# Three VectorE instructions instead of four to convert a float64 weight, and another place for the ScalarE one

## The chip, the core and the metric

The kernel runs on one core of a Trainium2 chip. The metric is the device time of one execution in microseconds (us). TensorE (PE) multiplies, its weight loads are listed as PEld; VectorE is DVE, ScalarE is ACT, GpSimd is POOL, and SP is the sequencer that issues almost every DMA. Each engine works through its own instructions in order and waits on semaphores.

## What is computed

An attention with a learned relative bias (batch 4, 8 heads, 576 positions, head size 64), then a gated convolution block, then a block that mixes tokens with a cosine and a sine of a linear map:

```python
scores = scale * q @ k.T + bias           # bias: a small MLP of log-distances, per head
x = softmax(scores) @ v                   # reshaped to (4, 576, 512)
gate = sigmoid(causal_conv5(x, conv_w))
x = (gate * (x @ w_val)) @ w_out          # called m1 below
theta = x @ w_theta                       # from here on: m2
y = w_tok_r @ (x * cos(theta)) + w_tok_i @ (x * sin(theta))
u = x + y
out = u + relu(u @ w_ch)
```

The weights of the last two blocks arrive as float64: `w_val`, `w_out`, `w_theta`, `w_ch` are 512 x 512, `w_tok_r` and `w_tok_i` 576 x 576, `conv_w` is 5 x 512. Nothing is converted on the host; the kernel gets the 64-bit words as pairs of 32-bit integers.

## The kernel before

**Weight conversion.** `f64_stages` (L68) returns the stages of one block of 128 rows. `raw` holds the words, low and high alternating. Stage 0 loads it (SP, L706 or L717). Stage 1 is ACT: the absolute value of the high words read as float32, into `f64a` (L82). Stage 2 is DVE: it sets to zero what is below `TINY` and takes the sign back (L85). Stage 3 shifts left by 5 and right by 2 (DVE, L91), stage 4 ors in the two top bits (DVE, L96), stage 5 ors in the top three bits of the low words (DVE, L101). The float32 in `f64h` is then split into a high part (ACT, L105) and a low part (POOL, L108), stages 6 and 7. There are 12 blocks of 512 columns and one of 20 (`conv_w`) in the attention, 9 of 576 (the token weights, into `wtok`) in m1, and 8 of 256 (`w_ch`) in m2. `raw` and `f64a` have two buffers, `f64h` has one.

**Bias and attention.** First 36 groups of bias are made and written to DRAM, until about 57 us. The attention then runs over 80 steps; a step is one query tile of 128 rows of one pair of heads and one batch, five steps (four tiles and a tail of 64 rows) are an iteration, and there are 16 iterations. The first ten steps are taken in the order of `FIRST`. The order of instructions is written out by hand in `attention` (L419), under a manual schedule. At step s: PE makes the scores (`qk`, L242) into two PSUM tiles; DVE adds the bias and finds the minimum (`soft`, L256); ACT exponentiates (L259); one step later DVE and POOL normalise (`norm`, L268 to L271); three steps later PE transposes (L301, and L314 for the rest), ACT and DVE copy the result out (`tr_out`, `mid_out`, L279 and L281), and PE multiplies by the values (L362, L372). ACT copies the finished output (`xst`, L382).

**Places of the weight stages.** The table `WS` says in which step a stage of which block is written: (iterations after the block's own, step of the iteration counted from 0, stage, place in the step). Place 0 is ahead of `norm`, place 1 behind it, place 2 at the step's end. One block starts in each iteration, 13 in all.

**m1 and m2.** Four convolution taps per row block on DVE (L532), the gates (L564), splits into high and low parts (L63 on ACT, L65 on POOL), and matmuls in triples (L114 to L116); `xo` (L578) is the copy of an output out of PSUM by ACT, and `x2d` is where it is stored. The first taps already run in the last 18 steps of the attention. In m1, `pace` spreads the stages of the nine token blocks over 70 slots in the order in which they are listed; in m2, eight stages of the `w_ch` blocks are written behind each token product. A list scheduler sets the final order there. The first token block's load waits for the end of the attention.

Of the kernel before, what the change touches and what calls it, by code (L numbers as in the profile page):

```python
# [2 lines left out]

# [7 lines left out]
F32 = mybir.dt.float32  # L11
F32R = mybir.dt.float32r
I32 = mybir.dt.int32
AF = mybir.ActivationFunctionType
ALU = mybir.AluOpType
# [13 lines left out]
BW, BR = 592, 608  # L29
BIG = 3.0e38  # L30

TINY = struct.unpack("f", struct.pack("I", 0x38100000))[0]

MAGIC = 12582912.0
INV2PI = 0.15915494309189535
# [32 lines left out]
def f64_stages(nc, alloc, n, load, hi, lo):  # L68

    t = {}

    def s0():
        t["raw"] = alloc("raw")
        load(t["raw"])

    def s1():  # L80
        t["a"] = alloc("f64a")
        nc.scalar.activation(out=t["a"][:, :n], in_=t["raw"][:, :n, 1].bitcast(F32), func=AF.Abs)  # L82

    def s2():
        nc.vector.scalar_tensor_tensor(out=t["a"][:, :n], in0=t["a"][:, :n], scalar=TINY,  # L85
                                       in1=t["raw"][:, :n, 1].bitcast(F32), op0=ALU.is_ge, op1=ALU.mult)

    def s3():
        t["h"] = alloc("f64h")
        x, h = t["a"][:, :n].bitcast(I32), t["h"][:, :n].bitcast(I32)  # L90
        nc.vector.tensor_scalar(out=h, in0=x, scalar1=5, scalar2=2, op0=ALU.logical_shift_left,  # L91
                                op1=ALU.logical_shift_right)

    def s4():
        x, h = t["a"][:, :n].bitcast(I32), t["h"][:, :n].bitcast(I32)
        nc.vector.scalar_tensor_tensor(out=h, in0=x, scalar=-(1 << 30), in1=h, op0=ALU.bitwise_and,  # L96
                                       op1=ALU.bitwise_or)

    def s5():
        h = t["h"][:, :n].bitcast(I32)  # L100
        nc.vector.scalar_tensor_tensor(out=h, in0=t["raw"][:, :n, 0], scalar=29, in1=h,  # L101
                                       op0=ALU.logical_shift_right, op1=ALU.bitwise_or)

    def s6():
        nc.scalar.activation(out=hi, in_=t["h"][:, :n], func=AF.Copy)  # L105

    def s7():
        nc.gpsimd.tensor_tensor(out=lo, in0=t["h"][:, :n], in1=hi.bitcast(F32), op=ALU.subtract)  # L108

    return [s0, s1, s2, s3, s4, s5] + ([s6, s7] if lo is not None else []), t  # L110


def mm3(nc, out, wh, wl, xh, xl, first, last):
# [5 lines left out]
class Kernel:  # L119
# [270 lines left out]
    def av_plan(self, j):  # L390
# [13 lines left out]
        if qt < 3:  # L404
# [4 lines left out]

    WS = ((2, 0, 5, 2), (2, 1, 6, 2), (2, 2, 7, 2), (0, 2, 0, 2), (0, 4, 1, 2), (1, 2, 2, 1), (1, 4, 3, 0),
          (1, 4, 4, 1))

    BL = {(B - 2, 1): 0, (B - 2, 3): 1, (B - 2, 4): 4, (B - 1, 1): 2, (B - 1, 3): 3}

# [2 lines left out]
    def attention(self, blocks, hooks):  # L419
# [5 lines left out]
        for s in range(NU + 4):  # L425
# [38 lines left out]
            def stages(place):  # L464
                for i, step, stage, pl in self.WS:
                    if s < NU and r == step and pl == place and 0 <= it - i < len(blocks):
                        blocks[it - i][stage]()
# [236 lines left out]
    def wblock(self, alloc, dram, w, kc, c0=0, n=DM):  # L704
        def load(raw):
            self.nc.sync.dma_start(out=raw[:, :n].rearrange("p a b -> p (a b)"),  # L706
                                   in_=dram[128 * kc:128 * kc + 128, c0:c0 + n].bitcast(I32))
        return f64_stages(self.nc, alloc, n, load, w[0][:, kc, c0:c0 + n], w[1][:, kc, c0:c0 + n])[0]

    def tokblock(self, alloc, kt):  # L710
        wr, wi = self.a["w_tr"], self.a["w_ti"]

        def load(raw):
            flat = raw.rearrange("p a b -> p (a b)")
            if kt < 8:
                w, r = (wr, kt) if kt < 4 else (wi, kt - 4)
                self.nc.sync.dma_start(out=flat, in_=w[128 * r:128 * r + 128, :].bitcast(I32))  # L717
            else:
                self.nc.sync.dma_start(out=flat[0:64], in_=wr[TM:S, :].bitcast(I32))
                self.nc.sync.dma_start(out=flat[64:128], in_=wi[TM:S, :].bitcast(I32))  # L720
        return f64_stages(self.nc, alloc, S, load, self.wtok[0][:, kt], self.wtok[1][:, kt])[0]
# [22 lines left out]
    def conv_block(self, alloc):  # L744
        n = KC * 5

        def load(raw):
            for c in range(KC):
                self.nc.sync.dma_start(out=raw[:, 5 * c:5 * c + 5].rearrange("p k b -> p (k b)"),
                                       in_=self.a["conv_w"][128 * c:128 * c + 128, :].bitcast(I32))  # L750
        stages, t = f64_stages(self.nc, alloc, n, load, None, None)
        return stages + [lambda: self.nc.vector.tensor_copy(out=self.cw.rearrange("p c k -> p (c k)"),
                                                            in_=t["h"][:, :n]), lambda: None]
# [304 lines left out]
```

## Time and profile before

| what | us |
|---|---|
| median of 3 runs (lowest, highest) | 625.67 (624.54, 626.31) |
| the profiled execution, its own time | 622.14 |
| its span, first to last instruction | 620.4 |
| PE busy | 597.4 (96%) |
| PEld busy | 459.2 (74%) |
| DVE busy | 477.1 (77%) |
| ACT busy | 393.8 (63%) |
| POOL busy | 321.3 (52%) |
| the four conversion lines on DVE, all shapes, L85 / L91 / L96 / L101 | 20.7 / 19.0 / 21.9 / 22.2 |

The span can be cut into four stretches: bias (0 to 57), attention (57 to 288), m1 (288 to about 395), m2 (to 620). In a timeline row the first number is the start in us, the second the time; a bracket at the end tells how long the engine had been idle before and what ended that. A busy engine in one stretch may be idle in the next, so the shares of the whole span decide nothing.

### The profile page before, as it was taken

What the parts mean: (1) busy time and instruction counts of PE and PEld (TensorE: products, weight loads), DVE (VectorE), ACT (ScalarE), POOL (GpSimd) and SP (SyncE); (2) the same over time, 40 slices, a digit from 0 to 9 for tenths busy, and PEclk for the clock granted to TensorE, in tenths of its full rate; (3) what the DMA queues carried; (4) which work ended last, traced back from release to release, by engine and by line L of the source; (5) the groups of instructions that cost most, each with busy time, mean ns of one, the idle gap of its engine ahead of it and who ended that gap; (6) DMA issues with size and microseconds to landing.
All of it is one profiled execution on the core that took longest, in us unless ns stands there. A gap on an engine that the chain in (4) does not pass through costs nothing.

```text
span 620.4 us, 14765 instructions
## 1 busy us (share of the span) xinstructions
PE 597.4 (96%) x5552; PEld 459.2 (74%) x5552; DVE 477.1 (77%) x1155; ACT 393.8 (63%) x869; POOL 321.3 (52%) x342
## 2 busy tenths in 40 slices
PE   5999899999999998989999999999999999999997
PEld 2334455555555554557989999879998999999997
DVE  7997799999999998787999997499977436416112
ACT  5998788888888887976577574687447332614010
POOL 4555466666765665675577864244773242125120
PEclk9999899999999998999999999999999999999999
DMA  6999589569748963202555636331234003001002
GB/s 178 279 326 264 155 224 257 178 179 235 172 143 233 260 193 89 78 21 60 158 166 180 207 110 229 110 103 35 71 94 142 2 11 144 1 0 49 30 1 78
DMA packets 51975, 84.42 MB, mean 136 GB/s; under 512 B 7472, under 2 KB 32176, under 8 KB 51392
## 3 DMA queue, kind: packets, MB, share of 16 engines
q1 hardware_dynamic: 51728, 83.12, 45.8%
q8 instruction: 44, 0.72, 0.5%
q10 hardware_dynamic: 144, 0.30, 0.1%
q14 instruction: 27, 0.22, 0.1%
q0 software_dynamic: 32, 0.07, 0.0%
HBM read 58.39 MB, written 25.07 MB: 135 GB/s over the span
## 4 chain that ended last, share of the span: by engine, by line
PE 71%; DVE 9%; ACT 8%; DMA 7%; issue 3%; POOL 1%; SPq 0%; ACTq 0%; DVEq 0%
PE mm L114 12%; PE mm L116 12%; PE mm L115 12%; PE o L362 10%; PE s L242 10%; PE t L301 6%; PE bp L177 4%; DMA qr<-x1d 3%; DVE ns L256 2%; DVE gs L532 1%; ACT ev L187 1%; ACT e L259 1%; PE o L372 1%; DVE raw L532 1%; DMA scr<-ev 1%
## 5 line engine op out<-in xcount | busy, mean ns | idle before, releaser
L271 POOL TENSOR_SCALAR e<-e,ri 128x576 f32<-128x576 f32 x144 | 118.3, 832 | 83.0 <-DVE ri L269 29.9
L259 ACT ACTIVATE e<-ns,mx 128x576 f32<-128x576 f32 x144 | 111.1, 772 | 29.3 <-DVE mx L256 19.3
L256 DVE CUSTOM_DVE_ANT_0 ns<-s,bias 128x576 f32<-128x576 f32 x128 | 93.7, 750 | 9.1 <-PE s L242 6.5
L242 PE MATMUL s<-kr,qr 64*128 64x288 f32 (+1 forms) x640 | 94.7, 432 | 0.4 <-DVE mx L256 0.4
L116 PE MATMUL mm<-wtok,zl 128*128 128x288 f32 x288 | 84.7, 295 | 0.8 <-POOL zl L65 0.8
L114 PE MATMUL mm<-wtok,zh 128*128 128x288 f32 x288 | 84.7, 295 | 0.0
L115 PE MATMUL mm<-wtok,zh 128*128 128x288 f32 x288 | 84.6, 294 | 0.0
L362 PE MATMUL o<-et,vm 128*64 128x320 f32 (+1 forms) x512 | 77.9, 427 | 0.0
L65 POOL TENSOR_TENSOR ul<-x,uh 128x288 fp32r<-128x288 f32 x32 | 26.8, 837 | 89.3 <-ACT uh L63 68.8
L301 PEld LDWEIGHTS t<-idt,e 64*128 64x128 f32 x1152 | 42.8, 140 | 38.5 <-POOL e L271 20.0
L680 DVE TENSOR_TENSOR x<-mm,x 128x288 f32<-128x288 f32 x32 | 14.5, 454 | 63.3 <-PE mm L116 63.3
L362 PEld LDWEIGHTS o<-et,vm 128*64 128x64 f32 x512 | 31.7, 138 | 38.5 <-issue 18.9
L279 ACT ACTIVATE et<-t 128x512 f32<-128x512 f32 (+1 forms) x103 | 53.7, 544 | 8.8 <-PE s L314 7.0
L242 PEld LDWEIGHTS s<-kr,qr 64*128 64x128 f32 (+1 forms) x640 | 47.6, 179 | 15.7 <-DVE mx L256 6.4
L63 ACT ACTIVATE uh<-x 128x288 fp32r<-128x288 f32 x32 | 14.1, 441 | 68.3 <-DVE x L680 68.3
L301 PE MATMUL t<-idt,e 64*128 64x64 f32 x1152 | 53.7, 230 | 2.3 <-ACT et L279 2.2
L116 PEld LDWEIGHTS mm<-wtok,zl 128*128 128x128 f32 x288 | 54.0, 188 | 1.0 <-POOL zl L65 1.0
L115 PEld LDWEIGHTS mm<-wtok,zh 128*128 128x128 f32 x288 | 54.0, 188 | 0.1
L114 PEld LDWEIGHTS mm<-wtok,zh 128*128 128x128 f32 x288 | 54.0, 188 | 0.1
L532 DVE SCALAR_TENSOR_TENSOR gs<-qr,cw,gs 128x288 f32<-128x288 f32 (+4 forms) x96 | 45.9, 510 | 3.2 <-ACT gs L528 3.2
L177 PE MATMUL bp<-h,w2n 128*32 128x512 f32 (+48 forms) x648 | 43.9, 404 | 2.4 <-DVE h L164 1.5
L164 DVE TENSOR_SCALAR h<-wpsi,nbp_i 128x577 f32<-128x577 f32 (+35 forms) x108 | 45.2, 494 | 0.0
(130 smaller groups left out, 1551.1 us busy)
## 6 DMA issues: line engine op xcount, KB each, us to landing
scr<-ev SPq DMA_DIRECT2D x36, 296.0 KB, 4.9
qr<-in_q SPq DMA_DIRECT2D x32, 288.0 KB, 4.6
bias<-scr SPq DMA_DIRECT2D x32, 288.0 KB, 7.5
vm<-in_v SPq DMA_DIRECT2D x16, 320.0 KB, 5.4
kr<-in_k SPq DMA_DIRECT2D x16, 288.0 KB, 5.1
x2d<-xo SPq DMA_DIRECT2D x8, 576.0 KB, 4.0
x<-x2d SPq DMA_DIRECT2D x4, 1152.0 KB, 6.0
out<-o SPq DMA_DIRECT2D x32, 144.0 KB, 1.7
```

The costliest lines, as they stand in the source:

```text
L114: nc.tensor.matmul(out=out, lhsT=wh, rhs=xh, start=first, stop=False)
L115: nc.tensor.matmul(out=out, lhsT=wh, rhs=xl, start=False, stop=False)
L116: nc.tensor.matmul(out=out, lhsT=wl, rhs=xh, start=False, stop=last)
L177: nc.tensor.matmul(out=ps[32 * c:32 * c + 32, n, o:o + hi - lo], lhsT=self.w2n, rhs=rhs, start=True, stop=True)
L242: nc.tensor.matmul(out=out, lhsT=w, rhs=k[r, e], start=True, stop=True)
L256: self.last_d = nc.vector.tensor_tensor_reduce(out=ns, in0=self.s4[e][:, :, :HALF], in1=bb.rearrange("p (n j) -> p n j", n=2), op0=ALU.add ...
L259: self.last_a = nc.scalar.activation(out=et[:, S * e:S * e + S], in_=ns.rearrange("p n j -> p (n j)"), func=AF.Exp, scale=-1.0, bias=mx[:, ...
L271: nc.gpsimd.tensor_scalar(out=et[:, S * e:S * e + S], in0=et[:, S * e:S * e + S], scalar1=ri[:, e:e + 1], scalar2=1.0, op0=ALU.mult, op1=A ...
L279: self.nc.scalar.activation(out=out, in_=in_, func=AF.Copy)
L301: self.nc.tensor.transpose(out=pt[h][:, 64 * kb:64 * kb + 64], in_=et[r, c:c + 128], identity=self.idt[r, r])
L362: nc.tensor.matmul(out=out, lhsT=vm[:, kb, 64 * e:64 * e + 64], rhs=rhs, start=(kb == 0), stop=(kb == 4))
L532: nc.vector.scalar_tensor_tensor(out=s[:, o:], in0=x[:, o + k:HALF + k], scalar=self.cw[:, m, k:k + 1], in1=s[:, o:], op0=ALU.mult, op1=AL ...
```

## The change

The ACT stage no longer takes the absolute value but multiplies the high words by 2 to the power -112, which rebiases the exponent. The compare and multiply (L85) is gone. What was a double shift is one shift by 3; the or that brought back the top two bits now brings the sign, read from `raw`; the or with the low words is as before. A block has seven stages instead of eight (five and the copy, instead of six and the copy, for `conv_w`).

The table has new places. With i the block's own iteration: the scaling on ACT moves from step 4 of i to step 1 of i + 1; the shift and the or with the sign stand where L91 and L96 stood (step 4 of i + 1); the or with the low words moves from the end of step 0 of i + 2 to step 1 of i + 2, behind `norm`; the load, the high part and the low part stay. In m1 and m2 fewer stages go over the same slots, and the scheduler's order of DVE, ACT, POOL and SP changes there. PE's order is the same from the first to the last instruction.

```diff
-TINY = struct.unpack("f", struct.pack("I", 0x38100000))[0]
+REBIAS = 2.0 ** -112
@@ f64_stages
     def s1():
         t["a"] = alloc("f64a")
-        nc.scalar.activation(out=t["a"][:, :n], in_=t["raw"][:, :n, 1].bitcast(F32), func=AF.Abs)
+        nc.scalar.activation(out=t["a"][:, :n], in_=t["raw"][:, :n, 1].bitcast(F32), func=AF.Copy, scale=REBIAS)
     def s2():
-        nc.vector.scalar_tensor_tensor(out=t["a"][:, :n], in0=t["a"][:, :n], scalar=TINY,
-                                       in1=t["raw"][:, :n, 1].bitcast(F32), op0=ALU.is_ge, op1=ALU.mult)
-    def s3():
         t["h"] = alloc("f64h")
         x, h = t["a"][:, :n].bitcast(I32), t["h"][:, :n].bitcast(I32)
-        nc.vector.tensor_scalar(out=h, in0=x, scalar1=5, scalar2=2, op0=ALU.logical_shift_left,
-                                op1=ALU.logical_shift_right)
+        nc.vector.tensor_scalar(out=h, in0=x, scalar1=3, scalar2=None, op0=ALU.logical_shift_left)
-    def s4():
-        x, h = t["a"][:, :n].bitcast(I32), t["h"][:, :n].bitcast(I32)
-        nc.vector.scalar_tensor_tensor(out=h, in0=x, scalar=-(1 << 30), in1=h, op0=ALU.bitwise_and,
-                                       op1=ALU.bitwise_or)
+    def s3():
+        h = t["h"][:, :n].bitcast(I32)
+        nc.vector.scalar_tensor_tensor(out=h, in0=t["raw"][:, :n, 1], scalar=-(1 << 31), in1=h, op0=ALU.bitwise_and,
+                                       op1=ALU.bitwise_or)
@@ class Kernel
-    WS = ((2, 0, 5, 2), (2, 1, 6, 2), (2, 2, 7, 2), (0, 2, 0, 2), (0, 4, 1, 2), (1, 2, 2, 1), (1, 4, 3, 0),
-          (1, 4, 4, 1))
+    WS = ((1, 1, 1, 0), (2, 1, 4, 1), (2, 1, 5, 2), (2, 2, 6, 2), (0, 2, 0, 2), (1, 4, 2, 0), (1, 4, 3, 1))
```

In the changed file every line behind the conversion stands a few lines higher (L259 is L253, L279 is L273, L256 is L250, L717 is L710).

ACT at steps 4 to 7, the first weight block. Rows are line, operation, tile written and tile read, size; `x2` is two in a row. Before:

```order
L259 ACTIVATE e,sm<-ns,mx 128x576
L82 ACTIVATE f64a<-raw 128x512
L259 ACTIVATE e,sm<-ns,mx 128x576
L279 ACTIVATE et<-t_1102 128x512
L279 ACTIVATE et<-t_1103 128x512
L259 ACTIVATE e,sm<-ns,mx 128x576 x2
L279 ACTIVATE et<-t_1149 128x512
L259 ACTIVATE e,sm<-ns,mx 128x576 x2
```

And now:

```order
L253 ACTIVATE e,sm<-ns,mx 128x576 x2
L273 ACTIVATE et<-t_1100 128x512
L273 ACTIVATE et<-t_1101 128x512
L253 ACTIVATE e,sm<-ns,mx 128x576 x2
L273 ACTIVATE et<-t_1147 128x512
L253 ACTIVATE e,sm<-ns,mx 128x576
L81 ACTIVATE f64a<-raw 128x512
L253 ACTIVATE e,sm<-ns,mx 128x576
```

The weight's activation has moved behind four exponentials and three copies.

DVE at steps 67 and 68, with a convolution tap in each step (L532 before, L525 now). Before:

```order
L268 TENSOR_SCALAR sm<-sm 128x2
L269 RECIPROCAL ri<-sm 128x2
L85 SCALAR_TENSOR_TENSOR f64a<-f64a,raw 128x512
L532 SCALAR_TENSOR_TENSOR bias<-bias,cw 128x286
L256 ISA ns,mx<-s_112,bias 128x576
```

And now:

```order
L262 TENSOR_SCALAR sm<-sm 128x2
L263 RECIPROCAL ri<-sm 128x2
L525 SCALAR_TENSOR_TENSOR bias<-bias,cw 128x286
L250 ISA ns,mx<-s_112,bias 128x576
```

The compare and multiply ahead of the tap is gone, and with it one instruction ahead of step 68's `soft`.

SP in the middle of m1: loads of token weights (`raw`) and stores of outputs (`x2d`). Before:

```order
L596 DMA xtail<-x2d_70 128x4x64
L580 DMA x2d_71<-xo 512x1x288
L717 DMA raw<-in_w_ti 128x1152
L493 DMA qr<-x1d_69 128x4x288
L592 DMA xt<-x2d_71 128x4x128 x2
```

And now:

```order
L589 DMA xtail<-x2d_70 128x4x64
L710 DMA raw<-in_w_ti 128x1152
L573 DMA x2d_71<-xo 512x1x288
L486 DMA qr<-x1d_69 128x4x288
L585 DMA xt<-x2d_71 128x4x128 x2
```

The weight load now stands ahead of a store that waits for ACT.

## Rows read from the trace of the kernel before

**Rows 1.** Stretch: length; busy us of PE, PEld, DVE, ACT, POOL; clock; DMA share, GB/s.

```profile
60.00:80.00 20.00, 17.40 (x196) 9.85 (x194) 15.22 (x51) 14.94 (x36) 9.97 (x15) 0.91 0.63 187
...
160.00:180.00 20.00, 20.00 (x240) 11.43 (x238) 19.62 (x60) 17.12 (x42) 13.18 (x17) 1.00 0.65 176
...
240.00:260.00 20.00, 18.46 (x204) 10.22 (x206) 16.00 (x46) 16.54 (x44) 12.02 (x15) 0.91 0.35 92
...
440.00:460.00 20.00, 20.00 (x154) 19.83 (x153) 17.06 (x27) 8.84 (x19) 17.18 (x17) 1.00 0.27 77
```

**Rows 2.** Timeline, steps 4 to 8: ACT and PE at the first weight block.

```profile
66.78 0.68 ACT L82 ACTIVATE f64a<-raw 128x512 f32<-128x512 f32 x1 [2.26 <-DMA raw<-in_w_val]
67.37 0.76 ACT L259 ACTIVATE e<-ns,mx 128x576 f32<-128x576 f32 x1
...
68.85 0.24 PE L301 MATMUL t<-idt,e 64*128 64x64 f32 x1 [1.35 <-ACT et L279]
...
69.94 1.17 PE L242 MATMUL s<-kr,qr 64*64 64x288 f32 x8
...
73.77 1.19 PE L242 MATMUL s<-kr,qr 64*128 64x288 f32 x8
```

**Rows 3.** Busy time: iterations 2 and 3 together, iteration 6, iteration 9.

```profile
78.45:105.85 27.40, 27.40 (x323) 15.42 (x320) 26.53 (x83) 22.72 (x56) 18.02 (x22) 1.00 0.93 232
132.52:145.86 13.34, 13.34 (x169) 7.66 (x166) 13.08 (x41) 11.74 (x29) 8.90 (x12) 1.00 0.92 242
172.53:185.85 13.32, 13.32 (x169) 7.63 (x166) 12.88 (x42) 11.29 (x29) 8.66 (x12) 1.00 0.53 154
```

**Rows 4.** Timeline: both ends of iteration 9 on PE, its L85 on DVE.

```profile
172.53 1.19 PE L242 MATMUL s<-kr,qr 64*128 64x288 f32 x8
...
180.85 0.18 DVE L85 SCALAR_TENSOR_TENSOR f64a<-f64a,raw 128x20 f32<-128x20 f32 x1
...
185.85 0.95 PE L242 MATMUL s<-kr,qr 64*128 64x288 f32 x6
```

**Rows 5.** Timeline, steps 33 to 35: ACT, and the weight load behind it.

```profile
142.50 0.78 ACT L259 ACTIVATE e<-ns,mx 128x576 f32<-128x576 f32 x1 [0.39 <-DVE mx L256]
...
144.01 0.74 PEld L362 LDWEIGHTS o<-et,vm 128*64 128x64 f32 x8 [0.44 <-ACT xst L382]
...
146.81 0.68 ACT L82 ACTIVATE f64a<-raw 128x512 f32<-128x512 f32 x1
...
148.38 0.78 ACT L259 ACTIVATE e<-ns,mx 128x576 f32<-128x576 f32 x1 [0.88 <-POOL e L271]
```

**Rows 6.** Timeline, step 67 to 69: L85 ahead of PE's longest wait.

```profile
236.40 0.67 DVE L85 SCALAR_TENSOR_TENSOR f64a<-f64a,raw 128x512 f32<-128x512 f32 x1
236.99 1.00 DVE L532 SCALAR_TENSOR_TENSOR bias<-bias,cw 128x286 f32<-128x286 f32 x1
...
238.76 0.78 ACT L259 ACTIVATE e<-ns,mx 128x576 f32<-128x576 f32 x1 [0.98 <-DVE mx L256]
...
240.60 0.28 PE L314 MATMUL s<-idt,e 64*128 64x64 f32 x2 [2.25 <-ACT em L279]
```

**Rows 7.** Timeline, steps 52 and 53.

```profile
194.51 0.67 DVE L85 SCALAR_TENSOR_TENSOR f64a<-f64a,raw 128x512 f32<-128x512 f32 x1
...
196.94 0.28 PE L314 MATMUL s<-idt,e 64*128 64x64 f32 x2 [0.37 <-DVE em L281]
```

**Rows 8.** L85 in m1: durations in ns, least/median/most.

```profile
L85 DVE SCALAR_TENSOR_TENSOR f64a<-f64a,raw x9: 743/985/1715, 301.5 to 383.3; 128x576 f32<-128x576 f32 x9
```

**Rows 9.** What PE waited for in m1 (us in total, times, longest).

```profile
PE mm L114 <- ACT xo L578: 1.7, 3, 0.8
PE mm L115 <- POOL bias L65: 0.6, 1, 0.6
PE mm L114 <- DVE gv L564: 0.5, 1, 0.5
```

**Rows 10.** ACT's waits for token weights in m1 (same columns).

```profile
ACT f64a L82 <- DMA raw<-in_w_ti: 7.0, 4, 3.1
```

More of the change, by code (lines that the diff above doesn't have):

```diff
@@ L1 @@
-import struct
 from contextlib import ExitStack
@@ L81, in s1 @@
         t["a"] = alloc("f64a")
-        nc.scalar.activation(out=t["a"][:, :n], in_=t["raw"][:, :n, 1].bitcast(F32), func=AF.Abs)
+        nc.scalar.activation(out=t["a"][:, :n], in_=t["raw"][:, :n, 1].bitcast(F32), func=AF.Copy, scale=REBIAS)
     def s2():
-        nc.vector.scalar_tensor_tensor(out=t["a"][:, :n], in0=t["a"][:, :n], scalar=TINY,
-                                       in1=t["raw"][:, :n, 1].bitcast(F32), op0=ALU.is_ge, op1=ALU.mult)
-    def s3():
         t["h"] = alloc("f64h")
         x, h = t["a"][:, :n].bitcast(I32), t["h"][:, :n].bitcast(I32)
-        nc.vector.tensor_scalar(out=h, in0=x, scalar1=5, scalar2=2, op0=ALU.logical_shift_left,
-                                op1=ALU.logical_shift_right)
+        nc.vector.tensor_scalar(out=h, in0=x, scalar1=3, scalar2=None, op0=ALU.logical_shift_left)
[3 more added lines that the diff above has]
+                                       op1=ALU.bitwise_or)
     def s4():
-        x, h = t["a"][:, :n].bitcast(I32), t["h"][:, :n].bitcast(I32)
-        nc.vector.scalar_tensor_tensor(out=h, in0=x, scalar=-(1 << 30), in1=h, op0=ALU.bitwise_and,
-                                       op1=ALU.bitwise_or)
-    def s5():
         h = t["h"][:, :n].bitcast(I32)
@@ L102, in s5 @@
                                        op0=ALU.logical_shift_right, op1=ALU.bitwise_or)
+    def s5():
+        nc.scalar.activation(out=hi, in_=t["h"][:, :n], func=AF.Copy)
     def s6():
-        nc.scalar.activation(out=hi, in_=t["h"][:, :n], func=AF.Copy)
-    def s7():
         nc.gpsimd.tensor_tensor(out=lo, in0=t["h"][:, :n], in1=hi.bitcast(F32), op=ALU.subtract)
-    return [s0, s1, s2, s3, s4, s5] + ([s6, s7] if lo is not None else []), t
+    return [s0, s1, s2, s3, s4] + ([s5, s6] if lo is not None else []), t
 def mm3(nc, out, wh, wl, xh, xl, first, last):
```

## The prediction

> **What bounds the kernel now.** I first took the busy time by stretch [rows 1], because the page's shares mix stretches with different limits. From 160 to 180 us, in the middle of the attention, PE is busy 20.00 of 20 us and DVE 19.62; both look like the bound. From 60 to 80 us PE is busy only 17.40 and its clock is down (0.91). From 440 to 460, where the last weights are converted in m2, PE is full again and DVE is not. So three questions decide: who sets the pace in the middle of the attention, what is lost at its two ends, and what PE waits for in m1.
>
> For the first I compared two iterations. In iteration 9 the block under conversion is the small one, so L85 takes 0.18 us [rows 4] instead of 0.67 [rows 7], and the two instructions behind it shrink too. From score product to score product it lasts 13.32 us, where iteration 6 with a full block lasts 13.34 [rows 3]. Half a microsecond less of DVE work bought 0.02. That is this change's cut, made by the kernel itself, and PE does not care: DVE only runs less far behind PE. So PE sets the pace there.
>
> The Trainium skill (Perfetto Trace Analysis, Identifying the Most-Contended Engine) says that matmul busy time does not tell how close to its limit PE is. By that rule the 20.00 proves nothing, and DVE with 98% would be the bound, which is the second rival below; the row of iteration 9 speaks against it.
>
> At the ends it is otherwise. In step 4 ACT reaches the first block's L82 before its load has landed and stands still for 2.26 us; the exponential behind it starts at 67.37 [rows 2]. PE then waits 1.35 us for a copy that stands behind it on ACT, and the scores of step 7 start at 69.94 and those of step 8 at 73.77. At steps 67 to 69 DVE also carries a convolution tap per step: L85 and the tap delay step 68's minimum, ACT waits 0.98 us for it, and PE 2.25 for ACT [rows 6]. In m1 PE waits 1.7 + 0.6 + 0.5 = 2.8 us in all [rows 9].
>
> **The change part by part.**
>
> *The scaling, two steps later, at the start.* ACT in the new order goes from the exponential of step 4 straight to that of step 5, so it is 2.26 us of waiting and 67.37 - 66.78 = 0.59 of work earlier, at most 2.85. PE ends the value product of step 6 at 68.85 - 1.35 = 67.50 and can go on at once with the transposes; from their start to the scores of step 7 it took 69.94 - 68.85 = 1.09, so these come at 68.6, not 69.94. In step 7 PE was slow: its clock fell to 1.2 GHz behind the wait (0.91 on the mean of the 20 us [rows 1]), and it stood behind ACT again. If PE's shorter idle time leaves the clock at 2.4 GHz, and with ACT 2 us ahead (the scaling, now at the end of step 6, takes back 0.59, its data long landed), a steady step of 13.34 / 5 = 2.67 puts the scores of step 8 at 71.3 instead of 73.77, 2.5 earlier. Both orders are full on PE from there on. Lower end: PE's own wait, 1.35. Upper end: 2.85. I take **2.4**.
>
> *L85 gone, in the attention.* In the steady iterations nothing: the cover is PE's own 13.3 us, and DVE waits for PE 0.6 us sooner. Iterations 2 and 3 last 27.40 us, 2 x 13.34 = 26.68 would be the steady pace; DVE is catching up there (26.53 busy), so of the 0.72 us too much [rows 3] I take **0.5** (0 to 0.7). In step 53 PE waits 0.37 us for DVE, which has L85 a little ahead on its queue [rows 7]: **0.4** (0 to 0.4). At step 67 L85 occupies 236.99 - 236.40 = 0.59 us right ahead of the tap, on the chain through ACT to PE's wait of 2.25 [rows 6]: **0.6**. What is late next there is the tap itself, 1.00. The clock also falls in this stretch (0.91 from 240 to 260 [rows 1]): (1 - 0.91) x 20 = 1.8 us of PE work, of which most came back if the wait were short enough to keep the clock up. I don't count on it, since 1.65 us of waiting remain. So 0 to 2.2.
>
> *The or with the low words, one step later.* It leaves step 0, where DVE is behind, for step 1 behind `norm`; the part that waits for it, L105 on ACT, is still a step's length away. It frees `raw` one step later too, so SP issues the next `raw` load about 2 us later, with bias loads queued behind; that load's user is now two steps later, and the bias tiles belong to the next pair of heads. Nothing.
>
> *The scaling in the steady iterations.* Its old place was idle time: the exponential behind L82 waits another 0.88 us for POOL at 148.38 [rows 5]. Its new place is step 1, where ACT works back to back until a gap of 0.39 us at step 33. 0.59 us go in, 0.2 come out: the copy `xst` would end 0.2 us later. PE's weight load behind it waits 0.44 us, by the profile for that copy [rows 5], but a load runs ahead of PE's matmuls and has some of that to spare. Between 0 and 0.2 for each of 12 iterations; I take **0**.
>
> *The new first operand of the or (`raw`, every second word).* L101 reads `raw` in the same way, and the totals of the two lines in the table ahead are as good as equal (22.2 and 21.9 us). Nothing.
>
> *m1.* DVE loses nine L85 of 985 ns at the median, 743 at the least [rows 8], 6.7 to 8.9 us. PE can win at most its 2.8 us of waiting [rows 9]. Two pieces are touched directly: the 0.5 behind a gate on DVE, and the longest ACT wait for a token weight, 3.1 us [rows 10], which sits ahead of the 0.8 us that PE waited for `xo`. In the new order of SP that load stands ahead of the store that held it. **1.3**, between -0.8 (the scheduler's new order makes one such stall more) and 2.8. In m2 PE is full while the last blocks are converted [rows 1]: nothing.
>
> Sum: 2.4 + 0.5 + 0.4 + 0.6 + 1.3 = 5.2 us. The profiled execution took 622.14, so 616.9. The median of the runs is 625.67, 3.5 above that one execution, and I take the difference over to it: **620.5 us**.
>
> **The rivals.**
>
> *Only the start gains.* m1's new order gives back what DVE wins and the small terms come to nothing: 2.4 alone is 623.3; with the low clock still there, 1.35, 624.3. For it: a scheduler, not a hand, orders m1, and ACT's other waits there stay. Against it: the load that moves ahead of a store. Chance 0.20.
>
> *DVE is the bound of the attention.* Then each full block gives 0.59 us, 12 x 0.59 = 7.1 in place of the 1.5 of the attention's three small terms: 625.67 - 5.2 - 5.6 = 614.9. For it: DVE at 98% [rows 1]. Against it: iteration 9. Chance 0.05.
>
> *ACT becomes the bound in steps 1 to 3, and the kernel is slower.* If `xst`, or a copy out of PSUM, is on PE's path with no slack, the scaling's 0.59 us come out in each of 12 iterations, 7.1 us. With 2.4 won at the start and nothing else it ends at 625.67 + 4.7 = 630.4. It decides from 0.43 us of loss per iteration on (5.2 / 12). For it: ACT's gap is smaller than what is put in. Against it: half a step later ACT waits again and has caught up, and nothing that the late exponentials feed is needed before the next step. Chance 0.07.
>
> **How the numbers follow.** My forecast, a gain of 3.5 to 9 us, has 0.68; only the start 0.20; DVE 0.05; ACT 0.07. The bounds of the terms add up to 0.55 (1.35 - 0.8) and 8.95 (2.85 + 0.7 + 0.4 + 2.2 + 2.8), so 616.7 to 625.1. I leave out the slower rival, the DVE rival and the last stretch of the small gains: **616.5 to 624.4**. About 0.3% (1.9 us) is what a measurement of this kernel can tell from no change. Faster by more than that: the forecast, the DVE rival and a part of the start-only case, 0.82. Within: 0.11. Slower: 0.07.
>
> **What the new profile would show.** Right: no ACT wait for `raw` near 65 us; PE's wait of 1.35 gone and the clock at 1.00 from 60 to 80; step 8's scores near 71.3; iterations in the middle still 13.3 us; PE's wait near 240 down from 2.25 to about 1.6; L85 absent and PE's waits in m1 near 1.5 us. Wrong: iterations of 13.5 us or more with PE waiting for ACT; iterations of 12.8 (DVE was the bound); new PE waits in m1 for `xo` or a split; or a start where PE is held by something else, such as the bias tiles' loads.

## The result, and the profile after

The changed kernel took 614.62 us at the median against 625.11 for the kernel before in the same comparison: a ratio of 0.9844, 95% interval 0.9806 to 0.9881, or 10.5 us less. The two profiled executions differ by less: 622.14 and 614.71 us, 7.43; their spans are 620.4 and 612.9. A later comparison, told below, gave 622.76 and 616.02, a ratio of 0.9885 (0.9852 to 0.9918). Over the 70 executions of before that were timed later the median is 622.8, over all 10 of the changed kernel 615.3, 7.5 us apart. So the gain is about 7 us (6.7 to 7.5), and the first 10.5 has some luck of the draw in it: the first four executions of before were long ones. The prediction said 620.5 us, 5.2 less, and 616.5 to 624.4. The sign was right; the time lies 1.9 us below the range. A gain of 7 us lies inside the 3.5 to 9 that was forecast, the 10.5 of this comparison above it.

The busy time by stretch, for the changed kernel. The first two stretches are those of [rows 1]; the other three are iterations 2 and 3, iteration 6 and iteration 9, as in [rows 3]. Columns: stretch; length; busy us of PE, PEld, DVE, ACT, POOL; granted clock; DMA share, GB/s.

```profile
60.00:80.00 20.00, 18.57 (x223) 11.00 (x222) 17.64 (x61) 16.58 (x41) 11.32 (x17) 1.00 0.76 207
240.00:260.00 20.00, 18.84 (x222) 11.01 (x222) 15.71 (x47) 17.52 (x44) 12.86 (x17) 1.00 0.27 82
75.55:102.38 26.83, 26.83 (x318) 15.49 (x318) 25.65 (x79) 22.15 (x55) 17.18 (x22) 1.00 1.00 238
128.87:142.12 13.25, 13.25 (x168) 7.63 (x166) 12.67 (x40) 11.52 (x29) 8.63 (x11) 1.00 0.92 241
168.63:181.88 13.25, 13.25 (x168) 7.62 (x166) 12.67 (x41) 11.17 (x29) 8.62 (x11) 1.00 0.54 156
```

The clock is 1.00 where it was 0.91 in both stretches. The starts of the iterations tell how much earlier the work stands. Step 10 begins at 75.55 instead of 78.45, a lead of 2.90 us (from the start of each profile); after iteration 3 it is 105.85 - 102.38 = 3.47, at step 30 3.65, and at step 50 (181.88 against 185.85) 3.97. An iteration in the middle lasts 13.25 us, not 13.34.

The start, in the timeline of the changed kernel (PE and ACT at steps 7, 8 and 10; columns as in [rows 2]):

```profile
68.04 0.72 PE L236 MATMUL s<-kr,qr 64*64 64x288 f32 x8
69.33 0.67 ACT L81 ACTIVATE f64a<-raw 128x512 f32<-128x512 f32 x1
70.31 1.19 PE L236 MATMUL s<-kr,qr 64*128 64x288 f32 x8
75.55 0.76 PE L236 MATMUL s<-kr,qr 64*128 64x288 f32 x4 [0.40 <-DMA kr<-in_k]
```

ACT's scaling runs at 69.33 without a wait, and the scores of step 8 start at 70.31, 3.46 us earlier than in [rows 2]. At step 10 PE waits 0.40 us for a load of keys; that was in this execution alone.

The end of the attention, steps 67 to 70, answering to [rows 6] (the tap on DVE is L525 now):

```profile
230.88 0.50 DVE L525 SCALAR_TENSOR_TENSOR bias<-bias,cw 128x286 f32<-128x286 f32 x1
...
231.16 1.56 POOL L265 TENSOR_SCALAR e<-e,ri 128x576 f32<-128x576 f32 x2 [1.21 <-ACT e L253]
...
234.16 0.28 PE L308 MATMUL s<-idt,e 64*128 64x64 f32 x2 [1.33 <-ACT em L273]
```

The tap takes 0.50 us, half of what it took, and PE's wait is 1.33, not 2.25. POOL's `norm` starts 0.28 us behind the tap's start here. In before it started 0.32 us ahead of it and took 1.93 us:

```profile
236.67 1.93 POOL L271 TENSOR_SCALAR e<-e,ri 128x576 f32<-128x576 f32 x2 [1.22 <-PE s L242]
```

In before a stretch at half clock (1.2 GHz) followed that wait. This is its row, with the clock in the third column from the right:

```profile
240.74:244.15 3.41, 3.41 (x18) 1.07 (x16) 2.46 (x8) 2.32 (x6) 1.53 (x3) 0.50 0.37 90
```

The changed kernel's profile has no such stretch in the attention. Near the end of the attention PE's last short wait there ends at 272.18 us, against 279.75 before, a lead of 7.57; these two rows are of before and of the changed kernel:

```profile
279.75 0.28 PE L314 MATMUL s<-idt,e 64*128 64x64 f32 x2 [0.17 <-ACT em L279]
```

```profile
272.18 0.27 PE L308 MATMUL s<-idt,e 64*128 64x64 f32 x2 [0.17 <-ACT em L273]
```

From there to the end both need the same: 620.4 - 279.75 = 340.65 and 612.9 - 272.18 = 340.72 us. In m1 PE waits as much as before [rows 9], now for one thing only (us in total, times, longest):

```profile
PE mm L108 <- ACT xo L571: 2.9, 4, 1.3
```

### The profile page after: what moved, and what is told of

It reads as the page before. It is cut to its first block, busy times and chain, and to the rows that moved or that the text cites. A ratio compares the mean times of both kernels' runs of the same rounds, so it can differ in the third digit from the quotient of the medians.

```text
span 612.9 us, 14738 instructions
## 1 busy us (share of the span) xinstructions
PE 592.1 (97%) x5552; PEld 457.7 (75%) x5552; DVE 457.5 (75%) x1125; ACT 393.1 (64%) x869; POOL 315.6 (51%) x342
## 4 chain that ended last, share of the span: by engine, by line
PE 72%; DVE 8%; ACT 7%; DMA 5%; POOL 4%; issue 3%; SPq 0%; ACTq 0%; DVEq 0%; POOLq 0%
PE mm L108 12%; PE mm L110 12%; PE mm L109 12%; PE s L236 11%; PE o L356 10%; PE t L295 6%; PE bp L171 4%; POOL bias L64 2%; DMA raw<-in_w_tr 2%; DVE gs L525 2%; PE o L366 1%; ACT e L253 1%; DVE raw L525 1%; ACT ev L181 1%; DVE ns L250 1%
## 5 line engine op out<-in xcount | busy, mean ns | idle before, releaser
L265 POOL TENSOR_SCALAR e<-e,ri 128x576 f32<-128x576 f32 x144 | 115.2, 811 | 78.8 <-DVE ri L263 28.8
L253 ACT ACTIVATE e<-ns,mx 128x576 f32<-128x576 f32 x144 | 110.7, 771 | 27.0 <-POOL e L265 14.5
L250 DVE CUSTOM_DVE_ANT_0 ns<-s,bias 128x576 f32<-128x576 f32 x128 | 93.9, 751 | 9.8 <-PE s L236 7.1
L236 PE MATMUL s<-kr,qr 64*128 64x288 f32 (+1 forms) x640 | 92.9, 424 | 0.8 <-DMA kr<-in_k 0.4
L356 PE MATMUL o<-et,vm 128*64 128x320 f32 (+1 forms) x512 | 76.0, 418 | 0.0
L273 ACT ACTIVATE et<-t 128x512 f32<-128x512 f32 (+1 forms) x103 | 53.8, 545 | 7.7 <-PE s L308 5.1
L525 DVE SCALAR_TENSOR_TENSOR gs<-qr,cw,gs 128x288 f32<-128x288 f32 (+4 forms) x96 | 44.9, 509 | 1.9 <-ACT gs L521 1.8
```

What stands on the lines that cost most here:

```text
L236: nc.tensor.matmul(out=out, lhsT=w, rhs=k[r, e], start=True, stop=True)
L250: self.last_d = nc.vector.tensor_tensor_reduce(out=ns, in0=self.s4[e][:, :, :HALF], in1=bb.rearrange("p (n j) -> p n j", n=2), op0=ALU.add ...
L253: self.last_a = nc.scalar.activation(out=et[:, S * e:S * e + S], in_=ns.rearrange("p n j -> p (n j)"), func=AF.Exp, scale=-1.0, bias=mx[:, ...
L265: nc.gpsimd.tensor_scalar(out=et[:, S * e:S * e + S], in0=et[:, S * e:S * e + S], scalar1=ri[:, e:e + 1], scalar2=1.0, op0=ALU.mult, op1=A ...
L273: self.nc.scalar.activation(out=out, in_=in_, func=AF.Copy)
L356: nc.tensor.matmul(out=out, lhsT=vm[:, kb, 64 * e:64 * e + 64], rhs=rhs, start=(kb == 0), stop=(kb == 4))
```

## The experiments

Much below goes by the **lead**: how many us earlier the scores of a step start than in the first profile of before. Step 6 comes up to 3.9 us later in one execution than in another, whatever the kernel (the last section says why), so the lead is counted from step 6 on. Worked out from PE's rows in each trace:

```
lead over before at step     8    10    20    50    54    65    70    79
changed kernel, first     3.36  2.80  3.37  3.87  4.45  4.64  7.92  7.47
changed kernel, again     3.36  3.37  3.65  4.08  4.66  4.85  8.14  7.70
move_scale                3.36  3.37  3.11  3.04  3.02  2.96  2.97  2.97
three_only                0.32 -0.22  0.10  0.60  1.19  1.39  4.11  3.85
move_or_back              3.36  3.37  3.67  4.17  4.75  4.96  7.44  6.61
tail_extra                3.36  3.37  3.65  4.10  4.68  4.87  5.94  5.34
no_sign                   3.36  3.36  4.23  4.99  5.57  6.01  9.62  9.32
```

**before_again.** No edit.

> The kernel before, unchanged, to see what its executions look like beside its first profile (span 620.4 us, mean clock 0.994, two stretches of 3.41 us at half clock, at 70 and 240 us). Its four earlier times lie at 623.3 to 626.3 us, 1 to 4 us above the profiled one, while those of the changed kernel lie around its profiled one; that is why the medians show 10.5 us and the profiles 7.4. If the clock explains it, the executions of 625 us have a granted clock near 0.989 (3 us more, at half clock for some 6 us more) and the short ones 0.994; if it is something else (a transfer, the launch), the clock stays 0.994 in all of them.

Median 622.84 us of 12 executions, 618.79 to 626.83; ratio 0.9995 (0.9966 to 1.0024). The profiled execution was a long one, 626.83, with a mean clock of 0.989. Over 70 executions of before, the time rises by 0.53 us for each 0.001 of clock missing, which accounts for 59% of its variance: the clock is most of it, not all. Where the clock goes is seen from this profile against the first one. PE's timeline and two stretches of the new one, and below them the first of these stretches in the first profile:

```profile
53.02 1.07 PE L177 MATMUL bp<-h,w2n 128*32 128x512 f32 x8 [2.25 <-ACT ev L187]
...
50.00:62.00 12.00, 9.37 (x132) 4.47 (x126) 6.10 (x20) 7.41 (x14) 3.90 (x4) 0.86 0.63 189
240.00:250.00 10.00, 7.75 (x60) 3.99 (x58) 7.23 (x18) 5.82 (x15) 5.21 (x6) 0.66 0.52 137
```

```profile
50.00:62.00 12.00, 10.56 (x149) 5.32 (x151) 7.56 (x23) 9.20 (x18) 6.39 (x7) 1.00 0.91 265
```

In the bias stage PE waits 2.25 us for ACT instead of 0.32, half clock follows for 3.41 us, and behind step 68 it lasts 6.83 instead of 3.41. The first three times of before (median 625.67) were on the long side of this spread.

**move_scale.** The kernel before, with one entry changed:

```diff
-    WS = (..., (0, 2, 0, 2), (0, 4, 1, 2), (1, 2, 2, 1), ...
+    WS = (..., (1, 1, 1, 0), (0, 2, 0, 2), (1, 2, 2, 1), ...
```

> The kernel before, with its four VectorE instructions, and only ScalarE's first step of a block moved from step 4 to step 1 of the next iteration. Theory (the gain is the sum of single waits): the start's part alone comes, the scores of step 10 start 2.5 to 2.9 us earlier than before; no gain in the steady iterations (-0.2 to 0 each); PE's wait of 2.25 us near 240 us and the half clock behind it stay. Gain 2.5 to 3 us over the profiled execution of before. Rival (the move gives all, by keeping the clock up): 6 us or more. Rival (ScalarE pays in the steady iterations): the lead of step 10 is lost again by step 64.

618.87 us against 622.99, a ratio of 0.9940 (0.9915 to 0.9964): 4.1 us, more than the 2.5 to 3 expected. The lead is 3.37 at step 10, 3.11 at step 20 and 2.97 at the end. So the start comes alone, larger than expected, and the scaling's new place on ACT costs 0.4 in all: 0.26 in iterations 2 and 3, and 0.15 behind them. At the end nothing changed; PE still waits 2.29 us at step 68:

```profile
241.46 0.28 PE L314 MATMUL s<-idt,e 64*128 64x64 f32 x2 [2.29 <-ACT em L279]
```

**three_only.** The changed kernel with both moved steps where they were:

```diff
-    WS = ((1, 1, 1, 0), (2, 1, 4, 1), (2, 1, 5, 2), ...
+    WS = ((2, 0, 4, 2), (2, 1, 5, 2), (2, 2, 6, 2), (0, 2, 0, 2), (0, 4, 1, 2), (1, 4, 2, 0), (1, 4, 3, 1))
```

> The changed kernel with three VectorE instructions, but with both moved steps back where they were: the scaling in step 4, the or of the low words in step 0. Theory of single waits: the start is as before (ScalarE waits 2.3 us for the load, PE 1.35, half clock at 70 us), the lead is 0.5 us after iteration 3, 1.0 after step 54; at steps 66 to 69 PE's wait falls from 2.25 by the 0.6 us of the missing instruction, which gives 0.6 if the clock still falls and 2.2 if it doesn't. In m1 nothing. Gain 1.5 to 3.5 us. Rival (the tail's gain is all due to the missing instruction): 3.3 us at steps 65 to 70 alone, 4.5 in all. Rival (VectorE work counts everywhere): 6 us.

620.36 us against 622.99, 0.9953 (0.9930 to 0.9977): 2.6 us. Nothing at the start, and 0.50 in the steady iterations 4 to 9, which were expected to give nothing. At steps 65 to 70 the lead grows by 4.11 - 1.39 = 2.72, where the changed kernel has 3.28: most of the tail's gain comes with the missing instruction. DVE and PE there:

```profile
235.93 0.50 DVE L525 SCALAR_TENSOR_TENSOR bias<-bias,cw 128x286 f32<-128x286 f32 x1
...
239.04 0.28 PE L308 MATMUL s<-idt,e 64*128 64x64 f32 x2 [1.16 <-ACT em L273]
```

The tap is at 0.50 us again, PE waits 1.16, and the clock stays at 1.00 behind it.

**move_or_back.** The changed kernel with the or of the low words in step 0:

```diff
-    WS = ((1, 1, 1, 0), (2, 1, 4, 1), (2, 1, 5, 2), ...
+    WS = ((1, 1, 1, 0), (2, 0, 4, 2), (2, 1, 5, 2), ...
```

> The changed kernel with only the or of the low words back in step 0. Theory of single waits: the start is kept (step 10 2.9 us earlier than before), iterations 2 and 3 give 0.5; the 0.05 to 0.09 us per steady iteration go, 0.5 in all; at step 66 VectorE is again 0.8 us later, so that the tap falls beside GpSimd's norm and PE waits about 2 us at step 68 instead of 1.33, with half clock behind it: 2 us lost. Slower than the changed kernel by 2 to 3 us. Rival (the place of the or does nothing, as the prediction had it): the same as the changed kernel within 0.5 us.

616.03 us against 622.99, 0.9884 (0.9851 to 0.9918); the changed kernel itself, in its second comparison, has 616.02 and 0.9885. At the median the place of this or makes no difference. My theory fell here twice: the steady gain stays (3.67 to 4.17 from step 20 to 50), and so does the short wait at step 68:

```profile
235.81 0.28 PE L308 MATMUL s<-idt,e 64*128 64x64 f32 x2 [1.40 <-ACT em L273]
```

In the profile it is not quite nothing: from step 65 to 70 the lead grows by 2.48 here and by 3.28 in the changed kernel, and 0.6 of the difference is left at step 75. Here the tap of step 65 stands right behind the or and takes 1.00 us; in the changed kernel (second row) it takes 0.50:

```profile
227.04 1.00 DVE L525 SCALAR_TENSOR_TENSOR bias<-bias,cw 128x284 f32<-128x284 f32 x1
```

```profile
225.59 0.50 DVE L525 SCALAR_TENSOR_TENSOR bias<-bias,cw 128x284 f32<-128x284 f32 x1
```

The rest of the lower lead at step 79 is half clock at another place, at a wait of 2.00 us at step 78.

**after_again.** No edit.

> The changed kernel, unchanged, beside the kernel before on the same chip. Theory (the spread of the times is the number of stretches at half clock; each costs PE about 1.7 us, and before has at least the two at 70 and 240 us that the change takes away): its times lie within 614 to 618 us, before's within 620 to 628, and the ratio of the medians is 0.985 to 0.989, a gain of 7 to 9.5 us, since before's profiled execution had only two stretches while a more usual one has three. Rival (the 7.4 us between the first two profiles is the whole gain and the rest was the choice of runs): 7.4 us or less.

616.02 us (614.72 to 619.86) against 622.76, 0.9885 (0.9852 to 0.9918): 6.7 us. The theory's ratio of 0.985 to 0.989 holds, but its 7 us or more do not; the rival's 7.4 us or less does, and the gain is nearer to what the profiles show. In the changed kernel's 10 executions the time falls by 0.63 us per 0.001 of clock, which accounts for 96% of the variance.

**tail_extra.** The changed kernel with one instruction more, in step 67 alone, behind `norm`, where L85 stood:

```diff
-    WS = (..., (0, 2, 0, 2), (1, 4, 2, 0), ...
+    WS = (..., (0, 2, 0, 2), (1, 2, 7, 1), (1, 4, 2, 0), ...
...
+                def extra():
+                    nc.vector.scalar_tensor_tensor(out=t12["a"][:, :DM], in0=t12["a"][:, :DM], scalar=-BIG,
+                                                   in1=t12["a"][:, :DM], op0=ALU.is_ge, op1=ALU.mult)
...
```

`t12` is the last of the thirteen blocks; the others have nothing in that place.

> The changed kernel with one VectorE instruction of the removed one's size put back, in step 67 alone, right ahead of the convolution tap (it multiplies the last weight block by one in place). Theory (the tail's gain comes from this one instruction, because it pushes the tap beside GpSimd's norm and lets PE wait long enough to lose the clock): PE's wait near 233 us goes from 1.33 to 2.2 us, half clock follows it for 3.41 us, and the kernel is 2 to 2.7 us slower than the changed one. Rival (0.6 us of work on the chain costs 0.6 us): wait 1.9 us, clock stays, 0.6 us slower. Rival (the tail needs all thirteen removed instructions): no difference.

618.31 us, against 622.76 for before (0.9927, 0.9901 to 0.9954) and 616.02 for the changed kernel: 2.3 us lost for 0.67 us of work. From step 65 to 70 the lead grows by 1.07 instead of 3.29. The rows are the two instructions on DVE, POOL's `norm` beside them, PE's wait, and the stretch at half clock:

```profile
233.23 0.67 DVE L842 SCALAR_TENSOR_TENSOR f64a<-f64a 128x512 f32<-128x512 f32 x1
233.82 1.00 DVE L525 SCALAR_TENSOR_TENSOR bias<-bias,cw 128x286 f32<-128x286 f32 x1
...
233.51 1.93 POOL L265 TENSOR_SCALAR e<-e,ri 128x576 f32<-128x576 f32 x2 [1.21 <-ACT e L253]
...
237.44 0.27 PE L308 MATMUL s<-idt,e 64*128 64x64 f32 x2 [2.26 <-ACT em L273]
...
238.56:241.98 3.42, 3.42 (x28) 1.94 (x26) 2.69 (x7) 1.79 (x6) 1.98 (x3) 0.50 0.83 190
```

The extra instruction delays the tap by 0.59 us and pushes it right beside POOL's `norm`, where it takes 1.00 us instead of 0.50, and the `norm` 1.93 instead of 1.56. PE's wait is 2.26 instead of 1.33, and half clock comes back. All of [rows 6] is there again, made by one instruction. Of the 2.2 us, 0.9 are the wait and the rest, 1.3, the clock.

**no_sign.** The changed kernel without the or of the sign in the attention's thirteen blocks, so that the weights converted there lose their signs:

```diff
-    WS = (..., (0, 2, 0, 2), (1, 4, 2, 0), (1, 4, 3, 1))
+    WS = (..., (0, 2, 0, 2), (1, 4, 2, 0))
```

> The changed kernel without the or of the sign in the thirteen blocks of the attention (the weights lose their signs there; m1 and m2 keep it). Two instructions of VectorE per block for what was four. Theory (the first instruction's removal gave 0.5 us in the steady iterations because VectorE's lag behind PE showed in the wait of single score products; that lag is now 0.8 us and short enough): steady iterations gain no more, less than 0.1 us each, at most 0.3 in all; after step 64 nothing. Within 0.5 us of the changed kernel. Rival (each VectorE instruction has a price in every iteration, as VectorE is the bound): 0.05 to 0.6 us per iteration again, 0.5 to 7 us in all.

614.61 us against 622.76, 0.9852 (0.9823 to 0.9881), 1.4 less than the changed kernel. The expectation fell: iterations 2 and 3 give another 0.6 us, the steady ones another 0.3 (3.65 to 4.08 became 4.23 to 4.99), steps 54 to 65 0.25 and the rest 0.5. Iterations 2 and 3, and iteration 6:

```profile
75.98:102.51 26.53, 26.53 (x323) 15.46 (x320) 24.86 (x79) 22.83 (x56) 16.76 (x22) 1.00 1.00 254
128.92:142.13 13.21, 13.21 (x169) 7.71 (x166) 12.07 (x39) 11.65 (x29) 8.39 (x11) 1.00 0.93 242
```

Iteration 6 goes from 13.34 (four instructions) over 13.25 (three) to 13.21 (two), while DVE's busy time falls by 0.4 to 0.6 each time. An instruction on DVE has a price in every iteration, but 0.04 to 0.09 us for 0.4 to 0.6 us of work.

**m1_ahead and before_m1_ahead.** The changed kernel, and the kernel before, with the loads of the token weights one block ahead:

```diff
-                todo = [f for kt in range(9) for f in self.tokblock(self.stage(stg), kt)]
+                blks = [self.tokblock(self.stage(stg), kt) for kt in range(9)]
+                todo = blks[0][:1]
+                for i, blk in enumerate(blks):
+                    todo += [f for nb in blks[i + 1:i + 2] for f in nb[:1]] + blk[1:]
```

> The changed kernel with the loads of the token weights in m1 issued one block ahead. Theory (PE's 2.9 us of waiting for ScalarE's output copies in m1 come from ScalarE standing still for these loads, 0.6 to 1.7 us each): these ScalarE waits go, PE's waits fall from 2.9 to 1 us or less, 2 us faster than the changed kernel. Rival (ScalarE is late there for other reasons: gates from VectorE, the order that the scheduler makes): the waits change place, and the time stays within 1 us.

613.70 us against 622.76, 0.9854 (0.9822 to 0.9887), 2.3 less than the changed kernel's 616.02; the profiled executions, both with the clock all but full, differ by 2.0 (613.34 and 615.35), or by 1.4 from the first profile of the changed kernel (614.71). PE's waits in m1 fell from 2.9 to 1.5 us, not to 1 or less:

```profile
PE mm L108 <- ACT xo L571: 1.0, 2, 0.6
PE mm L108 <- DVE gv L557: 0.5, 1, 0.5
```

That these waits came from ACT's waits for the loads, as the theory has it, isn't shown. The edit also changes the order of ACT and DVE that the scheduler makes. And in the changed kernel's profile the longest of PE's four waits, 1.26 us, ends with a copy `xo` that has two waits of ACT ahead of it, one for a load and, nearer, a longer one for a tap on DVE:

```profile
342.57 0.74 ACT L81 ACTIVATE f64a<-raw 128x576 f32<-128x576 f32 x1 [1.17 <-DMA raw<-in_w_ti]
344.81 0.41 ACT L533 ACTIVATE g<-gs 128x288 f32<-128x288 f32 x1 [1.50 <-DVE gs L525]
345.12 0.41 ACT L571 ACTIVATE xo<-mm 128x288 f32<-128x288 f32 x1
345.57 0.40 PE L108 MATMUL mm<-bias,wo 128*128 128x288 f32 x1 [1.26 <-ACT xo L571]
```

> The kernel before, with the loads of the token weights in m1 issued one block ahead, as was done to the changed kernel. It tells whether the nine instructions that the change takes from VectorE in m1 are worth anything there. Theory (ScalarE's waits for the loads set m1's end, VectorE's length doesn't): the same 2 us gain as on the changed kernel, PE's waits in m1 from 2.6 to 1 us. Rival (with the loads gone VectorE is the next limit, and before has 7 to 9 us more on it): gain 0.5 us or less, with PE waiting for gates (`gv`).

623.93 us against 622.47, 1.0012 (0.9989 to 1.0036): no gain. The waits, the first three in m1 and the last at the start of m2:

```profile
PE mm L114 <- ACT xo L578: 0.9, 2, 0.5
PE mm L115 <- POOL bias L65: 0.5, 1, 0.5
PE mm L114 <- DVE gv L564: 0.4, 1, 0.4
...
PE mm L116 <- POOL xl L65: 0.9, 1, 0.9
```

In m1 the waits fall from 2.8 to 1.8 us, and a new one of 0.9 behind it takes that back. So by these runs the change is worth something in m1 only together with the earlier loads. That DVE's length is the reason in before wasn't shown: the new wait is for POOL.

**mid_dve and both.** The changed kernel with the copies `em` on DVE to the end; and that with the earlier loads of m1:

```diff
-        eng = "d" if u < self.taps_from else "a"
+        eng = "d"
```

> The changed kernel with the copies `em` of the last 18 steps on VectorE instead of ScalarE, as in all earlier steps. Theory (PE's waits of 1.3, 1.1 and 1.5 us at steps 68, 73 and 78 come from the exponential of 0.77 us that stands ahead of the copy on ScalarE; VectorE is free right behind its minimum): the three waits fall by 0.5 to 0.8 us each, 1.5 to 2 us faster than the changed kernel. Rival (with a tap in each step VectorE has no room, its lag behind PE grows and PE waits for the minimum instead): the same or slower.

612.40 us against 622.47, 0.9857 (0.9835 to 0.9879). PE's waits from step 65 to the end of the attention, the changed kernel first, then this one:

```profile
PE s L308 <- ACT em L273: 4.1, 4, 1.5
PE s L308 <- DVE mx L250: 0.7, 1, 0.7
```

```profile
PE s L308 <- DVE mx L250: 2.9, 4, 1.2
PE s L308 <- DVE em L275: 0.3, 1, 0.3
```

4.8 us of waiting became 3.2. Both theories had a part: the waits for ACT are gone, and some came back as waits for DVE's minimum.

> The changed kernel with the copies `em` on VectorE to the end and the loads of m1 one block ahead. If the two gains are waits of PE in different places, they add up: 2 us of the loads and what the copies alone give. If the copies alone lose, this is slower than with the loads alone by the same amount.

612.08 us against 622.47, 0.9850 (0.9825 to 0.9875). The two don't add up: with the copies on DVE the earlier loads bring 0.3 us at the median, 0.8 between the spans of the profiled executions (610.1 and 609.3). Why is seen in mid_dve: there PE's waits in m1 are already at 1.4 us, all for gates on DVE and none for `xo`, without the loads moved:

```profile
PE mm L108 <- DVE gv L557: 1.4, 3, 0.7
```

ACT waits longer for the loads there than in the changed kernel (7.7 us against 4.5), which again speaks against these waits alone as the cause of PE's. `both` has the lowest median of this study, 3 to 4 us below the changed kernel and level with mid_dve.

## Why the prediction was wrong, step by step

The leads of the first profile beside the terms of the sum (us):

```
term                              predicted   first profile
scaling later, at the start          2.4        2.90
L85 gone, iterations 2 and 3         0.5        0.57
steady iterations 4 to 9             0          0.50
step 53                              0.4        0.58
steps 55 to 65                       0          0.20
steps 65 to 70, wait and clock       0.6        3.28
steps 70 to 79                       0         -0.45
m1 and m2                            1.3       -0.1
sum                                  5.2        7.5
```

**The start: the mechanism was right, the size too low.** ACT's wait for `raw` is gone, PE's 1.35 too, the clock is 1.00. I expected the scores of step 8 at 71.3; they came at 70.31. The range's upper end of 2.85 was too low: ACT's 2.85 us were not a cap, since the clock's loss (half clock for 3.41 us from 70.07 in before) came on top. In every other profile with the scaling moved the lead at step 10 is 3.37; the 0.40 us wait for keys hid half a microsecond of it.

**Step 67: the term that was most mis-sized, and it was in plain view.** The prediction took the 0.59 us of L85, named the tap as "late next" and left the clock out ("I don't count on it, since 1.65 us of waiting remain"). Both failed: 3.28 us came, more than the term's upper bound of 2.2. The tap got shorter by itself, 1.00 to 0.50 us, because it now starts ahead of POOL's `norm` and not 0.3 us into it; so the wait fell to 1.33, not 1.65, and the clock stayed up. The kernel before has both lengths of such a tap, 1.00 us at 236.99 and 0.50 at 253.41. tail_extra shows that one instruction there is worth 2.2 us, and three_only, without L85 in any block, gains 2.7 in these steps. The rest comes with the new place of the or with the low words (move_or_back). The Trainium skill (SBUF — State Buffer, Who interferes with whom) says that a VectorE instruction with two inputs in SBUF contends with a GpSimd one that reads SBUF. The rows of the tap (0.50 beside 1.00) and of the `norm` (1.56 beside 1.93) agree that they contend; they show both of them slowed, where the page has one wait for the other. Had I asked what else changes when the tap starts earlier, 0.5 us more would have come off the wait. Whether a wait of 1.65 there would have kept the clock up no run shows: waits of 1.5 us at step 78 went either way.

**The steady iterations: I read the right experiment in the wrong place.** Iteration 9, with its short L85, lasts 13.32 us, and from that I took that DVE's length costs nothing. But only L85 and, at its end, the shift are short there (DVE is busy for 12.88 us instead of 13.08 [rows 3], not half a microsecond less), and a lag of DVE at the end of an iteration is felt at the next one's step 1. So the row to read was in iteration 10. The kernel before, score products of steps 41 and 42 (iteration 8, full blocks), then 51 and 52 (iteration 10, behind the short one):

```profile
162.16 1.29 PE L242 MATMUL s<-kr,qr 64*128 64x288 f32 x8
...
165.00 1.19 PE L242 MATMUL s<-kr,qr 64*128 64x288 f32 x8
...
188.80 1.19 PE L242 MATMUL s<-kr,qr 64*128 64x288 f32 x8
...
191.55 1.19 PE L242 MATMUL s<-kr,qr 64*128 64x288 f32 x8
```

And step 41 of the changed kernel:

```profile
158.34 1.23 PE L236 MATMUL s<-kr,qr 64*128 64x288 f32 x8
```

Step 41 lasts 165.00 - 162.16 = 2.84 us, step 51 2.75, and the difference lies in the group of eight score products, 1.29 against 1.19: its second half waits for DVE, and the profile shows that as longer products (0.50 us instead of 0.40 for the fifth), not as idle time. That DVE's length has a price was there to be read, though not the price of L85 alone, since all four instructions are short behind step 51. Without L85 step 41 lasts 2.79 us, 0.05 less; the other 0.04 of the 0.09 per iteration lie at step 43, behind L85 (2.51 instead of 2.55). The Trainium skill (Perfetto Trace Analysis, Identifying the Most-Contended Engine: matmul busy time doesn't tell how near PE is to its limit) was right about the row of 100% busy. The second rival, with 0.59 us per block, was wrong in size: iteration 6 gave 0.09 for L85, 0.04 more for the sign's or.

**Iterations 2 and 3** came within their bounds of 0 to 0.7: 0.57, or 0.28 in the other profile, where no wait for keys stands ahead of them. **Step 53** gave 0.58, more than its bound of 0.4: the step lasts 2.51 us instead of 3.10, so PE's wait of 0.37 was only a part of what DVE's delay cost there.

**The or of the low words, and the scaling on ACT:** "nothing" for the first was right at the median (move_or_back: 616.03 beside 616.02), while the profile has 0.6 us for it at steps 65 to 75. The second, taken as 0 with a bound of 0.2 for each of 12 iterations, is 0.4 us in all (move_scale).

**m1: the mechanism was wrong.** I expected 1.3 us because DVE loses nine instructions and a load goes ahead of a store. Both happened, and PE waited 2.9 us where it had waited 2.8: its waits for a gate and for a split went, and those for ACT's output copies grew from 1.7 to 2.9 us. m1_ahead, which moves the loads, brought 1.4 to 2.3 us, so there is time to be had in m1. Which of ACT's waits keeps the copies late stays open: the loads, DVE's taps and the scheduler's order all differ between these runs.

**The step from the profile to the median** failed too. The profiled execution of before was 622.14 and three timings had a median of 625.67; I took the 3.5 us over to the changed kernel. They belonged to those executions of before: the changed kernel's median (614.62) and its profiled execution (614.71) agree. Without this step the prediction would have been 616.9, 2.3 us too high.

Of the rivals, "only the start gains" fell: the tail gave as much as the start. "DVE is the bound" gave the nearest time (614.9) for the wrong reason. "ACT becomes the bound" cost 0.4 of its 7.1 us.

## What to carry to other kernels

When an instruction ahead of another one goes, price the later one again at its new time: what it runs beside may have made half of its duration. Where a wait of the matmul engine is followed by a stretch at half clock, cost the two together: where the shorter wait keeps the clock, it pays more than the instruction was long (here 2.2 us for 0.67). And where the kernel makes your experiment itself, as with a smaller block, follow the effect to the step where it is felt, one iteration later if need be, before calling it nothing.

## What the runs showed of the hardware

- **The clock follows single waits, but not by their length alone.** After PE waits of 2.25, 2.26 and 2.29 us at step 68 half clock followed for 3.41 us or more; after 1.16, 1.33 and 1.40 there it did not. In tail_extra the stretch costs about 1.3 us beyond the wait. Between them it goes either way: 2.00 us at step 78 lost the clock, 1.99 and 2.09 in the bias stage (three_only and move_or_back) did not, and 1.5 us at step 78 lost it in two profiles (before_again, three_only) and kept it in the others. At step 6 a wait of 1.35 us lost it in the first profile of before, and one of 1.29 in before_again did not. What else decides stays open.
- **One wait in the bias stage makes much of the spread.** In the thirteen profiles it is 0.3 to 0.6 us in some and 2.0 to 2.4 in others, in code that is the same in all kernels here, and the longer ones (2.25 us and more) took the clock down behind them. Whether a kernel then loses more depends on its later waits; before has two, at steps 6 and 68, behind which the clock fell.
- **A VectorE instruction of 128x286 with two inputs takes 0.50 us where GpSimd's scaling of 128x576 starts 0.28 us behind it, and 1.00 where one has started 0.3 us ahead of it,** and the latter's pair takes 1.93 us instead of 1.56. Other taps behind a scaling that started about 0.3 us ahead take 0.71 to 1.00 us, so the length beside it varies.
